# Conversion steps in another order, and transfers moved between and along the issuing queues, in a gated linear attention and SoLU kernel

## The chip, the cores and the metric

The kernel runs on one core of a Trainium2 chip. The metric is the time of one execution on the device in microseconds (us). The kernel before took 368.15 us, the median of three runs (367.41 to 369.79).

A core has five engines that work at the same time, each through its own list of instructions in order: TensorE (PE in the profile, with its weight loads as PEld), VectorE (DVE), ScalarE (ACT), GpSimd (POOL) and SyncE (SP), which here only issues transfers (DMAs). ScalarE can issue transfers too.

## The reference, cut to what matters

```python
# attention: batch 4, heads 8, sequence 768, head dim 48
for t in range(S):
    state = alpha[:, :, t, :, None] * state + np.einsum('bhd,bhe->bhde', k[:, :, t], v[:, :, t])
    y[:, :, t] = np.einsum('bhd,bhde->bhe', q[:, :, t], state)
x = y.transpose(0, 2, 1, 3).reshape(B * S, H * D)          # 3072 tokens x 384
# feed-forward: w_in 384 x 1024, w_out 1024 x 384
h = x @ w_in
e = np.exp(h - h_max)
solu = h * e / (e.sum(-1) + 1e-9)
ln = (solu - mean) / np.sqrt(var + 1e-6) * g_ln
return ln @ w_out
```

The weights `w_in` and `w_out` arrive in float64; all else is float32. The output is float32.

## The kernel before, in words

The sequence of 768 is cut into six groups of 128 tokens, for all four batches at once (`g` 0 to 5). Within a group the recurrence is done in closed form: running products of `alpha` (scans on VectorE) scale the keys one way and the queries the other, `scores` multiplies them on TensorE, `masked` (L289) keeps the causal half, `read_values` (L361) multiplies with v, and `read_state` (L354) adds what the state from the earlier groups contributes. `next_state` and `decay` (L261, GpSimd) carry the state on. The feed-forward of a group is `up` (L397, eight products f = 0 to 7 with blocks of `w_in`), the activation (`up_act`: exponential L411 on ScalarE, product L412 on VectorE, square L415 on ScalarE) and `down` (L516, with `w_out`, two halves for each of four tiles of tokens).

The order of the work on each engine is written out by hand in the program text. Group 0's feed-forward, group 1's attention and the conversion of the weights overlap in the stretch from about 28 to 100 us, and it is this stretch that the change touches.

**Conversion.** Weights come in eight pieces, 0 to 3 of `w_in`, 4 to 7 of `w_out`. `fetch(i, slot)` loads the raw words of piece i into a slot of `room` (L588). `bit(i, k)` does step k of piece i, all on VectorE but one:

- k = 0 (L632) and k = 1 (L636) build the upper part from the high words
- k = 2 (L640) takes its exponent
- k = 3 (L644) brings in the low words, after which the slot is free of VectorE
- k = 4 (L646) adds both into the weights; for piece 7 it is on GpSimd

The list `steps` holds the pairs (i, k) from piece 1 on, and `convert(n)` issues the next n of it. Five go ahead of the products, then after each product f of group 0 as many as its tuple says. Pieces share their work buffers with every second piece. ScalarE checks the range of each piece (`in_range`, L611 and L614), and scales `w_out` with the gains (`scaled`, L653), before `mean` (L667) multiplies it with ones.

**Loads.** `load(alpha, an, 1)` (L134) brings alpha of group 1, which ScalarE's `alpha_over` (L196, both halves) and VectorE's `alpha_T` (L179, L182) read. `load_v(1)` (L176) follows on the same queue.

**Transfers within SBUF.** Queries of group 1 are in two tiles: `qv`, the first 32 of the 48 dimensions of each head, and `qe`, the last 16. `read_state` and `decay` want them in another layout, `q64` (in the tile `lot`). `move_lasts` (L232) does eight transfers from `qe`, issued by SyncE, and `move_firsts` (L237) four from `qv`, issued in group 1 by ScalarE, in later groups by SyncE. The decay of the state (L261) reads the last column of `q64` from both.

The compiler of the program puts a wait on an instruction where it needs another's result. Transfers signal their landing on eight completion counters, shared by all queues, and a transfer also waits until the previous one on its counter has landed.

Of the kernel before, what the change touches and what calls it, by code (L numbers as in the profile page):

```python
# [32 lines left out]
def fast_path(ctx, tc, q, k, v, alpha, moe_w_in, moe_w_out, moe_g_ln, out):  # L33
# [12 lines left out]
    nc = tc.nc  # L46
    B, H, S, D = q.shape
# [6 lines left out]
    E0, E1 = 32, 16  # L54
# [44 lines left out]
    an = const.tile([P, H, TQ, D], FP, name="an")  # L99
    qn = const.tile([P, H, TQ, D], FP, name="qn")  # L100
# [11 lines left out]
    q64 = lot[:, 0 : 2 * H * SW].rearrange("p (c h t) -> p c h t", c=2, h=H)  # L112
# [8 lines left out]
    qv = const.tile([P, 2 * H, SW], FP, name="qv")  # L121
# [9 lines left out]
    def load(src, dst, g):  # L131
        t = slice(g * P, (g + 1) * P)
        for b in range(B):
            nc.sync.dma_start(  # L134
                out=dst[32 * b : 32 * b + 32].rearrange("t h u d -> t h (u d)"),
                in_=src[b, :, t, :].rearrange("h (t u) d -> t h (u d)", u=TQ),
            )
# [5 lines left out]
    def load_first(src, dst, g):  # L143
        t = slice(g * P, (g + 1) * P)
        for b in range(0, B, 2):
            nc.sync.dma_start(
                out=by_token(dst)[:, b : b + 2].rearrange("p b h d -> p (b h) d"),
                in_=src[b : b + 2, :, t].rearrange("b h p d -> p (b h) d"),
            )

    def ends_of(src, tag=None):

        ends = ring.tile([P, T4], FP, name=tag) if isinstance(tag, str) else lots[tag][:, 0:T4]
        ends = ends.rearrange("p (b d) -> p b d", b=B)
        nc.scalar.copy(out=ends.rearrange("p b (h d) -> p b h d", h=H), in_=by_token(src)[:, :, :, E0:D])
        return ends
# [12 lines left out]
    def held(x, n):  # L169

        return x[:, n, 0 : H * HW].rearrange("p (h e) -> p h e", e=HW)[:, :, E1:HW]

    def load_v(g):
        t = slice(g * P, (g + 1) * P)
        for b in range(B):
            nc.sync.dma_start(out=held(vn, b), in_=v[b, :, t, :].rearrange("h p d -> p h d"))  # L176
# [54 lines left out]
            for k in range(2):  # L231
                nc.sync.dma_start(out=q64[64 * i + E0 : 64 * i + 64, c, k::2], in_=qe[32 * b : 32 * b + 32])  # L232

    def move_firsts(queue=nc.sync):
        for b in range(B):
            i, c = divmod(b, 2)
            queue.dma_start(out=q64[64 * i : 64 * i + E0, c], in_=qv[32 * b : 32 * b + 32, 0:H])  # L237

    def ends_of_decay(copy=nc.gpsimd.tensor_copy):
        copy(out=qe[:, :, P:SW], in_=h4[:, H:NB, 1:2])  # L240
# [124 lines left out]
    def next_state(g):  # L365
        kv = banks("kv", [H, D], 2)
        for h in range(H):
            for c in range(2):
                for r in range(4):
                    b = 2 * (r // 2) + c  # L370
                    nc.tensor.matmul(
                        kv[c][quarter(r), h], lhsT=kg[:, b, h, E0 * (r % 2) : E0 * (r % 2) + E0],
                        rhs=vn[:, b, HW * h + E1 : HW * h + HW], start=True, stop=True,
                        tile_position=(0, 32 * r), skip_group_check=True,
                    )
        for c in range(2):
            s = held(state, c)
            if g == 0:
                nc.scalar.copy(out=s, in_=kv[c])
            else:  # L380
                nc.vector.tensor_tensor(out=s, in0=s, in1=kv[c], op=ALU.add)
# [8 lines left out]
    def up_mm(g, f):  # L390
        d = gr[g]
        h = ps_h.tile([P, T4], FP, tag="h", name="h")
        w = T4 if g or f < 2 else T4 // 2 if f == 2 else T4 // 4
        for a in range(KC):
            x = d["x"][:, a].rearrange("p b t -> p (b t)")
            for c in range(0, T4, w):
                nc.tensor.matmul(  # L397
                    h[:, c : c + w], lhsT=w_in[:, a, f * P : (f + 1) * P], rhs=x[:, c : c + w],
                    start=not a and not c, stop=(a == KC - 1), skip_group_check=True,
                )  # L400
        d["h"] = h

    def up_act(g, f, between=None):
        d = gr[g]
        h = d["h"]
        if g:
            e, u2 = (ring.tile([P, T4], FP, name=x) for x in ("e", "u2"))
        else:
            e, u2 = (sT[:, f % 4, 4 * i : 4 * i + 4].rearrange("p b t -> p (b t)") for i in range(2))
        u = u_of(g, f)  # L410
        nc.scalar.activation(out=e, in_=h, func=AF.Exp)  # L411
        nc.vector.tensor_tensor(out=u, in0=h, in1=e, op=ALU.mult)  # L412
        if between:
            between()
        nc.scalar.activation(out=u2, in_=u, func=AF.Square)  # L415
        d[f] = e, u2
# [16 lines left out]
    def array_sums(g, half):  # L433


        d = gr[g]
        if half == 0:
            d["q"] = [ps_a.tile([P, T4], FP, tag=f"a{i}", name=f"quarters{i}") for i in range(2)]
        for i in range(2):
            for f in range(4):  # L440
                r = quarter(f)
                nc.tensor.matmul(
                    d["q"][i][r], lhsT=ones[:, 0:32], rhs=d[4 * half + f][i], start=half == 0, stop=half == 1,
                    tile_position=(0, r.start), skip_group_check=True,
                )
        if half:
            d["p"] = one.tile([P, 2, T4], FP, name="p")
            for i in range(2):
                nc.scalar.copy(out=d["p"][:, i], in_=d["q"][i])
            d["unit"] = small_ones  # L450
# [125 lines left out]
    def fetch(i, slot, n=1):  # L576

        kind, f = pieces[i]
        w = n * F // (2 if kind else KC)
        raw = room[:, 1536 * slot : 1536 * (slot + n)].bitcast(U32)  # L580
        raw = raw.rearrange("p (m c f w) -> p c m f w", m=n, f=w // n, w=2)
        if kind:
            parts = [(slice(0, P), c, moe_w_out[(f + c) * P : (f + c + 1) * P, :]) for c in range(2)]
        else:
            parts = [(slice(0, P), c, moe_w_in[c * P : (c + 1) * P, f * P : f * P + w]) for c in range(KC)]
        for rows, c, src in parts:
            if float64:
                nc.sync.dma_start(  # L588
                    out=raw[rows, c].rearrange("p m f w -> p m (f w)"),
                    in_=src.bitcast(U32).rearrange("p (m x) -> p m x", m=n),  # L590
                )
            else:
                dst = w_out[rows, f + c, 0:DM] if kind else w_in[rows, c, f * P : f * P + w]
                nc.sync.dma_start(out=dst, in_=src)
        for m in range(n):
            raws[i + m] = raw[:, :, m]
# [19 lines left out]
    def bits(steps):  # L616
        for x in steps if float64 else ():
            bit(*x)
# [114 lines left out]
    for i in (0, 2, 1):  # L733
        if i == 1:
# [3 lines left out]
            out=qe[:, :, 0:P] if i == 2 else qv[:, part, 0:P], in0=t[i], in1=aT[:, part, 1:SW], op=ALU.mult  # L738
# [13 lines left out]
    keys_back(0)  # L752
    in_range(0)

    steps = [(1, 0), (1, 1)]
    for i in range(1, 8):
        steps += [(i, 2), (i + 1, 0), (i, 3), (i + 1, 1), (i, 4)]
    steps = [x for x in steps if x[0] < 8]
    for a, b in (((2, 1), (1, 4)), ((6, 1), (5, 4))):
        i, j = steps.index(a), steps.index(b)  # L760
        steps[i], steps[j] = b, a

    def convert(n):
        bits(steps[:n])
        del steps[:n]
# [4 lines left out]
    def check(f):  # L770
        for i, part in checks.get(f, ()):
            in_range(i, (part,))
        if f == FC - 2:
            scaled(4)

    for f in range(FC):
        up_mm(0, f)
        if f == 4:
            array_sums(0, 0)
        up_act(0, f, lambda: check(f))  # L780
        convert((5, 2, 3, 3, 4, 3, 2, 8)[f])
        if f == 0:
            next_state(0)
            fetch(4, 3)
            load(k, kn, 1)
            load_first(q, qn, 1)
        elif f == 1:
            fetch(5, 1)
        elif f == 3:
            fetch(6, 2)  # L790
            load(alpha, an, 1)
            ends_q = ends_of(qn, "u2")
        elif f == 5:
            fetch(7, 3)
            load_v(1)
        elif f == 6:
            scaled(5)
# [34 lines left out]
    for i in range(2):  # L832
        scan_on(1, i)
        part = slice(NP * i, NP * i + NP)
        nc.vector.tensor_tensor(out=qv[:, part, 0:P], in0=tq[i], in1=aT[:, part, 1:SW], op=ALU.mult)  # L835
    move_firsts(nc.scalar)
    down(2, 0)
    scores(1, 0)
    decay(1)
# [6 lines left out]
    masked(1)  # L846
    gr[0]["rest"]()
    finish(0)
    load(q, qn, 2)
    finish(1)  # L850
    finish(2)
    down(3, 0)
# [156 lines left out]
    def compare(out, x, bound, op):  # L1009
# [6 lines left out]
        out=chunks[:, :, 2], in0=sums[:, :, 2], scalar=0.25, in1=sums[:, :, 3], op0=ALU.mult, op1=ALU.is_le  # L1016
# [6 lines left out]
    else:  # L1023
# [9 lines left out]
        out=bad, in0=all_ok[0:1, 0:1], scalar1=float(P * ends[-1]), scalar2=None, op0=ALU.is_lt  # L1033
# [451 lines left out]
```

## Time and profile before

| what | us |
|---|---|
| median of the runs | 368.15 |
| the profiled execution | 368.27 |
| its span, from the first to the last instruction | 366.5 |
| TensorE busy | 355.9 (97%) |
| VectorE busy | 243.7 (67%) |
| ScalarE busy | 146.4 (40%) |
| GpSimd busy | 132.7 (36%) |

In the lines of the timelines below, the first number is the start in us from the span's start and the second the length; then come the engine, the line, the operation, what is written and what is read, the shapes and the number of instructions. A bracket gives the idle time of the engine just ahead, and what ended it. In the list of waits, a line gives the engine, the line that waited and what it waited for, then the total in us, how often, and the longest. `SPq` and `ACTq` are the issuing of transfers by SyncE and ScalarE. The row of busy times has, for each engine, the time, its share of the span and the number of instructions.

### The profile page before, as it was taken

How to read it: one execution, taken by the hardware profiler on the slowest of the kernel's cores; microseconds unless marked ns; L12 is line 12 of the kernel's file. 1: busy time of each engine (PE TensorE's matmuls, PEld its weight loads, DVE VectorE, ACT ScalarE, POOL GpSimd, SP SyncE). 2: the span in 40 equal slices, each digit the busy share in tenths (PEclk: the TensorE clock that was granted, in tenths of full speed). 3: DMA queues.
4: the chain of work that ended last, by engine and by line, in shares of the span. 5: the costliest groups of instructions: out<-in, count | busy, mean ns of one | idle time of the engine just before them, and what ended most of it. 6: DMA issues, size and time to landing. Idle time of an engine off the chain costs nothing. (4 is left out here: it accounts for less than half of the span.)

```text
span 366.5 us, 10048 instructions
## 1 busy us (share of the span) xinstructions
PE 355.9 (97%) x4341; PEld 222.8 (61%) x4341; DVE 243.7 (67%) x381; ACT 146.4 (40%) x261; POOL 132.7 (36%) x128
## 2 busy tenths in 40 slices
PE   8999999988999999999999999999999999999994
PEld 8876896555665566556484556575556565545552
DVE  0999889999987696935765946766956403445420
ACT  2648787327646361252431243531242222322110
POOL 7020002004358673764232763332773120233300
PEclk9999999999999999999999999999999999999999
DMA  9995994723596609354044354004032000000011
GB/s 181 185 323 143 230 253 90 171 53 75 146 208 138 140 6 197 84 131 115 3 109 91 104 113 112 24 26 88 21 88 74 0 25 1 23 21 22 23 47 50
DMA packets 70216, 36.06 MB, mean 98 GB/s; under 512 B 44169, under 2 KB 66961, under 8 KB 70161
## 3 DMA queue, kind: packets, MB, share of 16 engines
q1 hardware_dynamic: 68944, 33.87, 40.3%
q10 hardware_dynamic: 1216, 1.45, 1.4%
q8 instruction: 36, 0.59, 0.7%
q14 instruction: 20, 0.16, 0.1%
HBM read 25.30 MB, written 4.72 MB: 82 GB/s over the span
## 5 line engine op out<-in xcount | busy, mean ns | idle before, releaser
L516 PE MATMUL o<-w_out,room 128*128 128x385 f32 x384 | 133.4, 491 | 0.0
L397 PE MATMUL h<-x,w_in 128*128 128x512 f32 (+2 forms) x384 | 132.1, 490 | 0.0
L516 PEld LDWEIGHTS o<-w_out,room 128*128 128x128 f32 x384 | 71.3, 190 | 55.1 <-issue 13.2
L397 PEld LDWEIGHTS h<-x,w_in 128*128 128x128 f32 x384 | 62.4, 190 | 50.6 <-issue 41.8
L412 DVE TENSOR_TENSOR room<-h,e 128x512 f32<-128x512 f32 x40 | 27.7, 691 | 74.0 <-ACT e L411 74.0
L411 ACT ACTIVATE e<-h 128x512 f32<-128x512 f32 x40 | 23.9, 598 | 100.3 <-PE h L397 100.3
L430 POOL TENSOR_TENSOR p<-p,e 128x512 f32<-128x512 f32 x30 | 43.1, 1437 | 20.0 <-ACT e L411 19.9
L415 ACT ACTIVATE u<-room 128x512 f32<-128x512 f32 x40 | 25.2, 630 | 35.2 <-DVE room L412 35.2
L555 POOL TENSOR_TENSOR r<-sums,mhalf 128x1 f32<-128x1 f32 x20 | 14.8, 741 | 66.3 <-DVE sums L546 66.0
L289 DVE TENSOR_TENSOR sT<-a,mask 128x512 f32<-128x512 f32 x43 | 26.7, 686 | 6.8 <-PE a L278 6.7
L204 DVE TENSOR_TENSOR_SCAN hT<-aT,unit 128x516 f32<-128x516 f32 x18 | 24.3, 1400 | 7.9 <-ACT aT L719 7.9
L225 POOL TENSOR_TENSOR kT<-kT,hT 128x1024 f32<-128x1024 f32 (+1 forms) x8 | 13.3, 1684 | 33.5 <-DVE kT L179 33.5
L278 PEld LDWEIGHTS a<-qv,kT 32*128 32x128 f32 x704 | 20.8, 186 | 7.6 <-issue 2.4
L204 DVE TENSOR_TENSOR_SCAN aT<-aT,seed 128x516 f32<-128x516 f32 x18 | 24.8, 1407 | 0.2
L430 DVE TENSOR_TENSOR p<-p,u 128x512 f32<-128x512 f32 x30 | 21.5, 717 | 5.1 <-ACT u L415 5.1
L333 PE MATMUL y<-sT,vn 128*32 128x128 f32 x768 | 23.4, 274 | 0.9 <-issue 0.7
L278 PE MATMUL a<-qv,kT 32*128 32x128 f32 x704 | 23.2, 277 | 1.1 <-DVE qv L835 0.8
L333 PEld LDWEIGHTS y<-sT,vn 128*32 128x32 f32 x768 | 20.9, 110 | 2.9 <-issue 2.2
L196 ACT ACTIVATE sq<-an,mone 128x1536 uint8<-128x1536 f32 x12 | 18.9, 1571 | 0.2
L557 ACT ACTIVATE o_sb<-o,r 128x384 f32<-128x384 f32 x16 | 9.3, 580 | 18.5 <-POOL r L555 18.5
L646 POOL TENSOR_TENSOR w_out<-lot 128x768 f32<-128x768 f32 x1 | 1.8, 1847 | 37.2 <-DVE lot L644 37.2
L261 POOL TENSOR_TENSOR state<-state,lot 128x384 f32<-128x384 f32 x10 | 8.8, 900 | 16.7 <-DMA lot<-qe 13.3
(148 smaller groups left out, 378.0 us busy)
## 6 DMA issues: line engine op xcount, KB each, us to landing
vn<-in_v_dram SPq DMA_DIRECT2D x24, 192.0 KB, 4.6
kn<-in_k_dram SPq DMA_DIRECT2D x20, 192.0 KB, 4.9
an<-in_alpha_dram SPq DMA_DIRECT2D x20, 192.0 KB, 4.2
out_dram<-o_sb SPq DMA_DIRECT2D x20, 192.0 KB, 1.9
room<-in_moe_w_out_dram SPq DMA_DIRECT2D x8, 384.0 KB, 6.0
qn<-in_q_dram SPq DMA_DIRECT2D x16, 192.0 KB, 3.5
lot<-qe SPq DMA_DIRECT2D x40, 64.5 KB, 2.1
lot<-qv SPq DMA_DIRECT2D x16, 129.0 KB, 2.4
```

Of the source, the lines that this page charges most:

```text
L196: nc.scalar.activation(out=sq, in_=x, func=AF.Relu, scale=1.0 - 2 * i, bias=mone, accum_out=over[:, g, i : i + 1])
L204: nc.vector.tensor_tensor_scan(out=o, data0=a, data1=s, initial=1.0, op0=ALU.mult, op1=ALU.add)
L278: nc.tensor.matmul(a[b][:, i], lhsT=kT[quarter(b), kb], rhs=qv[quarter(b), qb, 0:P], start=not last and not i, stop=bool(last), tile_posit ...
L289: nc.vector.tensor_tensor(out=sT[:, b, half * NP : half * NP + NP], in0=a[b], in1=mask[:, None, :].to_broadcast([P, NP, P]), op=ALU.mult,)
L333: nc.tensor.matmul(y_bank(b)[quarter(r), a], lhsT=lhsT, rhs=rhs, start=(b, r) not in begun, stop=stop, tile_position=(row, 32 * r), skip_g ...
L397: nc.tensor.matmul(h[:, c : c + w], lhsT=w_in[:, a, f * P : (f + 1) * P], rhs=x[:, c : c + w], start=not a and not c, stop=(a == KC - 1), ...
L411: nc.scalar.activation(out=e, in_=h, func=AF.Exp)
L412: nc.vector.tensor_tensor(out=u, in0=h, in1=e, op=ALU.mult)
L415: nc.scalar.activation(out=u2, in_=u, func=AF.Square)
L430: eng.tensor_tensor(out=p, in0=d[0][i] if f == 1 else p, in1=d[f][i], op=ALU.add)
L516: nc.tensor.matmul(d["o"][:, 0 : DM + 1], lhsT=u_of(g, f)[:, b * P : b * P + P], rhs=w_out[:, f], start=(f == 0), stop=(f == FC - 1), skip ...
L555: nc.gpsimd.tensor_tensor(out=r, in0=s[:, 3:4], in1=mhalf, op=ALU.pow)
```

## The change

Four things. The list of conversion steps is written out in a new order, and the numbers of steps per product go from (5, 2, 3, 3, 4, 3, 2, 8) to (5, 2, 3, 4, 3, 3, 3, 7). In steps per product, where 43 is piece 4 with k = 3:

| behind product | before | after |
|---|---|---|
| 3 | 41 34 42 | 41 34 42 43 |
| 4 | 50 43 51 44 | 44 50 51 |
| 5 | 52 60 53 | 52 60 53 |
| 6 | 54 61 | 54 61 62 |
| 7 | 62 70 63 71 64 72 73 74 | 63 70 71 64 72 73 74 |

Those ahead are the same. Second, alpha's load for group 1 goes from behind `fetch(6, 2)` (product 3) to behind `fetch(7, 3)` (product 5). Third, `move_firsts` of group 1 is issued by SyncE. Fourth, the load of the queries of group 2 goes from behind the first output's transfer (`finish(0)`) to just behind `move_firsts`.

```diff
-    def move_firsts(queue=nc.sync):
+    def move_firsts():
         for b in range(B):
             i, c = divmod(b, 2)
-            queue.dma_start(out=q64[64 * i : 64 * i + E0, c], in_=qv[32 * b : 32 * b + 32, 0:H])
+            nc.sync.dma_start(out=q64[64 * i : 64 * i + E0, c], in_=qv[32 * b : 32 * b + 32, 0:H])
...
-    steps = [(1, 0), (1, 1)]
-    for i in range(1, 8):
-        steps += [(i, 2), (i + 1, 0), (i, 3), (i + 1, 1), (i, 4)]
-    steps = [x for x in steps if x[0] < 8]
-    for a, b in (((2, 1), (1, 4)), ((6, 1), (5, 4))):
-        i, j = steps.index(a), steps.index(b)
-        steps[i], steps[j] = b, a
+    steps = [10, 11, 12, 20, 13, 14, 21, 22, 30, 23, 31, 24, 32, 40, 33, 41, 34, 42, 43, 44, 50, 51, 52, 60, 53, 54, 61, 62]
+    steps = [divmod(x, 10) for x in steps + [63, 70, 71, 64, 72, 73, 74]]
...
-        convert((5, 2, 3, 3, 4, 3, 2, 8)[f])
+        convert((5, 2, 3, 4, 3, 3, 3, 7)[f])
...
         elif f == 3:
             fetch(6, 2)
-            load(alpha, an, 1)
             ends_q = ends_of(qn, "u2")
         elif f == 5:
             fetch(7, 3)
+            load(alpha, an, 1)
             load_v(1)
...
-    move_firsts(nc.scalar)
+    move_firsts()
+    load(q, qn, 2)
     down(2, 0)
     scores(1, 0)
     decay(1)
...
     gr[0]["rest"]()
     finish(0)
-    load(q, qn, 2)
     finish(1)
     finish(2)
```

## The prediction, made before the result was known

> **What bounds the kernel now.** I read the page first, then TensorE's own timeline from 24 to 100 us (the change touches nothing outside), then the timelines of the engines that TensorE waits for there, and last SyncE's waits.
>
> ```profile
> PE 355.9 (97%) x4341; PEld 222.8 (61%) x4341; DVE 243.7 (67%) x381; ACT 146.4 (40%) x261; POOL 132.7 (36%) x128
> ...
> 73.43 0.66 PE L303 MATMUL tp<-ident,kT 128*128 128x128 f32 x4 [0.92 <-DVE kT L817]
> 73.92 2.76 PE L516 MATMUL o<-w_out,room 128*128 128x385 f32 x8
> 77.50 2.07 PE L278 MATMUL a<-qv,kT 32*128 32x128 f32 x64 [0.82 <-DVE qv L835]
> ...
> 84.28 2.86 PE L516 MATMUL o<-w_out,room 128*128 128x385 f32 x8
> 87.52 0.55 PE L333 MATMUL y<-lot,state 64*32 64x128 f32 x16 [0.38 <-POOL state L261]
> 88.75 1.02 PE L333 MATMUL y<-lot,state 64*32 64x128 f32 x48 [0.68 <-POOL aT L188]
> 89.70 1.56 PE L516 MATMUL o<-w_out,room 128*128 128x385 f32 x4
> ```
>
> Columns: start, length, then in brackets the idle time ahead and what ended it. TensorE is the bound. From 24 to 72.5 us it has no gap, so whatever becomes faster there buys nothing there. Its stalls sit in three places: 0.92 us before the last key transposes, 0.82 us before the scores, and around `read_state(0)`. The third is priced by starts. From 84.28 to 89.70 pass 5.42 us; the same `down` elsewhere lasts 2.76 (73.92 to 76.68) and `read_state` 1.26 from start to start (123.65 to 124.91 in the next group), 4.02 in all, so the stall is 1.40 us. Together 3.14 us: **the most that the change can win here**.
>
> The first two stalls end with VectorE, which works through `keys_T(1)` to `masked(1)` almost without a pause from 61.56 us. So what counts is when it gets there, and the conversion ahead has pauses:
>
> ```profile
> 45.43 0.69 DVE L412 TENSOR_TENSOR room<-h,sT 128x512 f32<-128x512 f32 x1 [0.71 <-ACT sT L411]
> 46.87 0.56 DVE L632 TENSOR_SCALAR lot<-room 128x768 uint32<-128x768 uint32 x1 [0.75 <-DMA room<-in_moe_w_out_dram]
> ...
> 55.57 0.69 DVE L412 TENSOR_TENSOR room<-h,sT 128x512 f32<-128x512 f32 x1 [0.80 <-ACT sT L411]
> 56.18 0.55 DVE L640 TENSOR_SCALAR lot<-lot 128x768 uint32<-128x768 uint32 x1
> 57.00 0.56 DVE L632 TENSOR_SCALAR lot<-room 128x768 uint32<-128x768 uint32 x1 [0.26 <-DMA room<-in_moe_w_out_dram]
> ...
> 61.56 2.19 DVE L179 STREAM_TRANSPOSE kT<-kn 128x1024 f32<-128x1024 f32 x1
> ```
>
> The third stall ends with GpSimd's `decay(1)`, which waits for transfers within SBUF:
>
> ```profile
> 75.64 10.64 SPq L232 DMA_DIRECT2D lot<-qe  x8
> 79.38 2.53 ACTq L237 DMA_DIRECT2D lot<-qv  x4
> 86.63 0.84 POOL L261 TENSOR_TENSOR state<-state,lot 128x384 f32<-128x384 f32 x1 [12.93 <-DMA lot<-qe]
> 87.86 0.84 POOL L261 TENSOR_TENSOR state<-state,lot 128x384 f32<-128x384 f32 x1 [0.39 <-DMA lot<-qe]
> ...
> SPq L232 <- DMA lot<-qv: 5.4, 1, 5.4
> ```
>
> Of `move_lasts`' eight issues the first is at 75.64 and the second only at 81.79: SyncE sits 5.4 us until the first of ScalarE's `move_firsts` has landed (79.38 + 2.4). The two write different partitions; the wait is on a completion counter. The program of before has eight of these for all transfers, dealt out in the order in which it expects the transfers to start, and a transfer waits for its counter's previous user. `move_firsts` got its counters first.
>
> **What the Trainium skill says.** Perfetto Trace Analysis, Identifying the Most-Contended Engine: matmul busy share misleads, since matmuls are pipelined. Agreed: TensorE shows as 97% busy and the `read_state` stall shows as 1.06 us of gaps where starts give 1.40; I use starts. DMA: Bandwidth & Descriptors, Issuing engines are not separate DMA queues: ScalarE's and SyncE's transfers share the same engines, and a second issuer saves issue time only. Agreed: `lot<-qv` lands after a median 2.4 us from either queue. Same page, Anatomy of one DMA: a semaphore wait is served by the issuing sequencer before dispatch. Agreed: all seven later `move_lasts` stood behind the second's wait. SBUF — State Buffer, Who interferes with whom: a VectorE operation with two SBUF inputs is held up by a GpSimd one that reads SBUF. Agreed: L543 took 0.72 us instead of 0.16 and ended with the second decay, at 88.71.
>
> **The change, part by part.** Starts follow each other on VectorE by 0.47 us for L632 and L640, 0.87 for L636, L644 and L646 (40.16, 40.63; 42.43, 43.30, 44.17), and by 0.60 for L412. I name steps by piece and k.
>
> (1) *Steps.* No instruction more or less: 43 goes from behind product 4 to behind product 3, 44 then stands ahead of 50, 62 goes from behind 7 to behind 6, and 63 ahead of 70. Behind product 3, 43 fills the 0.71 us pause: it starts at 44.63 and ends its 0.87 at 45.50, so L412 of product 4 slips from 45.43 to 45.5. Then 44 (to 46.97), 50 without its 0.75 us wait, since its data landed at 46.8, 51, done at 48.3. Product 5's L412 now waits for its exponential (49.14) and starts at 49.17 instead of 49.96. Steps 52, 60, 53 end at 51.6; product 6's exponential is ScalarE's and stays (52.03), so the lead shrinks: L412 at 52.06 instead of 52.36. 54, 61, 62 end at 54.87; `scaled(5)` waits for 54 and starts 0.3 earlier, so product 7's exponential ends at 55.22, and L412 is at 55.25. Before, 70, 63, 71, 64, 72, 73 took 4.56 (57.00 to 61.56, 74 being GpSimd's); the same six, in their new order and with no wait for 70, now start at 55.85. `keys_T(1)` starts at 60.41: **1.15 us earlier**.
>
> (2) *alpha behind w_out's last.* Piece 7 goes into piece 4's room, so its load waited for 43 (48.30); now 43 ends at 45.6 and ScalarE's range check of piece 4 at 46.3. It is issued at 46.3 instead of 48.36. Alpha's four follow at about 47.1 to 49 instead of 43.71 to 46.7; behind them on SyncE only `load_v(1)`, from 49.3 as before, needed after 90. The engines are full in these slices (DMA share about 1), so bytes come in order: before, alpha's last landed at 45.64 + 9.6 = 55.2 and w_out's last at 48.75 + 8.2 = 57.0. Exchanged, w_out's is there by about 53.5 (70 needs it at 56.7) and **alpha at about 57.0**. Its first reader is `alpha_over` on ScalarE, at 56.5: it waits 0.5 us. Behind it there are the copies of p, `scaled(6)` and `scaled(7)`. TensorE wants p at 61.0 and the last scaled rows at 64.7; from alpha's landing these take 1.75 + 1.05 = 2.8 and about 6.7 us, so alpha may land as late as 58.0 at no cost. I take nothing; beyond 58.0 it is us for us.
>
> (3) *All within SBUF by SyncE.* The eight lasts go at 0.65 us each, as in the next group (112.41 to 117.58): from 74.5 (VectorE's lead) to 79.7. The four firsts wait for L835's second, 79.30 less 1.15, so they follow at once, at 0.6 to 0.8 each (3.23 for four in the next group), and land by 83.6 (third) and 84.6. `decay(1)` ends at 84.5 and 85.5 instead of 87.47 and 88.70. TensorE, itself 1.15 earlier, gets to `read_state(0)` at 85.9: **the 1.40 us go**, with 0.7 to spare. ScalarE loses its 3.7 us wait and 2.5 us of issues; it had idle time there, so nothing. What is late next: nothing behind the firsts but the queries' load.
>
> (4) *Next queries' load.* Four issues move from 91.02 to about 82.5, behind the firsts; its first reader is at 97.83, so no gain, and the outputs' issues no longer stand behind it. If it met the firsts' packets it could cost `decay` some tenths, which the 0.7 cover.
>
> *Sum.* The key stall: 0.92 shrinks to nothing. TensorE then stands before the scores until VectorE's 76.35 instead of 77.50: 1.15 won in all by there (0.59 of the 0.82 stays). Plus 1.40: 2.55 us. VectorE must follow: its 1.15, and 0.56 of L543's hold-up, give 1.7 at 100 us, with a pause of 0.71 ahead of L412 at 101.54 to spare; enough. One term works against: `decay(2)` ends at 123.92 and TensorE reads at 123.65, nothing to spare. Its chain begins with alpha's third load behind ScalarE's `alpha_over`, which follows TensorE, so it moves along; it may give back 0 to 0.5 us. I take 0.1.
>
> The profiled execution took 368.27 us, of which the span is 366.5. 366.5 - 2.45 = 364.05 span, 365.8 with the 1.77 around it; the median of the runs is 0.12 below the profiled one, so **about 365.7 us**, 0.7% less.
>
> **Rivals.** (A) *Half of it*: the conversion lead is eaten by ScalarE (its order, not VectorE's, sets products 6 and 7), or the firsts on SyncE come too late for `decay(1)`, or `decay(2)` takes back what is won. For it: the lead already shrinks from 0.79 to 0.30 at product 6, and the 0.7 us margin. Against: the removed waits for data are real. Gain 0.9 to 1.5: 367.0. (B) *Slower*: alpha lands late. Its packets share the engines with v's, issued right behind, and `alpha_over` blocks ScalarE, thus p, the row sums on TensorE, then `scaled(7)` and the mean of w_out. It costs from 58.0 on and outweighs the gain from 60.5 on; at 61.5, where v's own last now lands (60.1) and somewhat beyond, the loss is 1.0: 369.2. Against it: v is queued behind alpha, and w_out's last, in the same place before, was not held up past 57.0. (C) *More*: VectorE's lead is over 1.7 us, so that the score stall goes too: 3.1 us, 365.1. Against: ScalarE's exponentials. That the change doesn't do what it says can't be, save that the counters are dealt out anew: were the lasts again to wait for later transfers, (A).
>
> **Chances.** Forecast (gain 1.7 to 2.9) 0.62; A 0.22; B 0.08; C 0.08. The forecast's own range, with 0.5 us for the median of a few runs, is 364.6 to 366.9. To leave out no more than 2 in 10 it reaches to A's end and some of C: 364.3 to 367.8. One per cent, about what tells a change from none here, is 3.7 us, more than all three stalls; only C with luck in the runs gets there: faster 0.08, slower 0.03, the same 0.89.
>
> **What would show it.** Right: `keys_T(1)` at 60.2 to 60.7; no wait ahead of L303's last four; the lasts in one row of 5.2 us and the firsts behind, from SyncE; `decay(1)` over before TensorE's L333; TensorE's first L397 of the next group, 98.14 before, at about 95.6. Wrong: `alpha_over` starting after 58; a wait of SyncE within the lasts; an L333 that waits for `state` near 86 or 121.

## The result, and the profile after

| | before | after |
|---|---|---|
| median of 8 runs each, us | 368.41 | 365.19 |
| lowest to highest, us | 366.42 to 369.79 | 364.67 to 365.89 |
| the profiled execution, us | 368.27 | 364.92 |
| its span, us | 366.5 | 363.1 |

The ratio after to before is 0.9919, with a 95% interval of 0.9893 to 0.9945: 0.8% faster, where 0.7% was forecast (365.7 us, range 364.3 to 367.8). The interval has 1% in it.

The first part of the page of the kernel after, engine by engine:

```profile
PE 354.5 (98%) x4341; PEld 221.8 (61%) x4341; DVE 243.4 (67%) x381; ACT 146.4 (40%) x261; POOL 132.8 (37%) x128
```

No engine has more or fewer instructions than before. What changed is when TensorE stood. Its own timeline:

```profile
71.07 1.66 PE L303 MATMUL tp<-ident,kT 128*128 128x128 f32 x12
72.57 2.76 PE L516 MATMUL o<-w_out,room 128*128 128x385 f32 x8
76.15 2.07 PE L278 MATMUL a<-qv,kT 32*128 32x128 f32 x64 [0.82 <-DVE qv L830]
...
82.93 2.86 PE L516 MATMUL o<-w_out,room 128*128 128x385 f32 x8
85.72 1.16 PE L333 MATMUL y<-lot,state 64*32 64x128 f32 x64
86.82 1.56 PE L516 MATMUL o<-w_out,room 128*128 128x385 f32 x4
```

The twelve key transposes are one row now: the bracket ahead of the last four is gone. The 0.82 us ahead of the scores stands, to the hundredth. And `read_state(0)` (L333) follows the `down` ahead of it with no bracket.

To compare kernels, I take differences between starts on TensorE in one execution. The landmarks are: the first sums over the products (L442, "product sums" below and "first down" in the expectations of e9 to e11; their start is the zero, since all of TensorE's work before it is untouched by the change), the `down` behind the key transposes, the scores, the `down` ahead of `read_state(0)`, the one behind it, the one behind `read_values`, and the L397 behind `read_state` of group 2.

| stretch, us | before | after | difference |
|---|---|---|---|
| product sums to `down` behind key transposes | 30.21 | 29.25 | -0.96 |
| on to the scores | 3.58 | 3.58 | 0 |
| on to the `down` ahead of `read_state(0)` | 6.78 | 6.78 | 0 |
| on to the `down` behind it | 5.42 | 3.89 | -1.53 |
| on to the `down` behind `read_values` | 7.04 | 6.49 | -0.55 |
| on to L397 behind `read_state` of group 2 | 28.17 | 28.45 | +0.28 |
| all | 81.20 | 78.44 | -2.76 |

The last matmuls start 3.29 us earlier (353.46 to 350.17). Of the rest, 0.39 us was there before the first changed instruction ran (L442 at 43.71 and 43.32), and so is no work of the change.

VectorE's timeline, the conversion steps up to the transposes of the keys:

```profile
44.37 0.96 DVE L644 SCALAR_TENSOR_TENSOR lot<-room,lot 128x768 f32<-128x768 uint32 x1
45.24 0.68 DVE L412 TENSOR_TENSOR room<-h,sT 128x512 f32<-128x512 f32 x1
...
48.78 0.69 DVE L412 TENSOR_TENSOR room<-h,sT 128x512 f32<-128x512 f32 x1 [0.53 <-ACT sT L411]
...
51.66 0.69 DVE L412 TENSOR_TENSOR room<-h,sT 128x512 f32<-128x512 f32 x1 [0.38 <-ACT sT L411]
...
54.89 0.69 DVE L412 TENSOR_TENSOR room<-h,sT 128x512 f32<-128x512 f32 x1 [0.20 <-ACT sT L411]
...
60.20 2.18 DVE L179 STREAM_TRANSPOSE kT<-kn 128x1024 f32<-128x1024 f32 x1
```

The two pauses for w_out's data, 0.75 and 0.26 us, are gone. Step 43 (44.37) fills the pause ahead of L412, and what is left are three short waits for ScalarE's exponential. The key transposes start at 60.20 instead of 61.56; from the product sums it is 16.88 instead of 17.85 us, so 0.97 earlier.

Then SyncE's and GpSimd's timelines:

```profile
74.29 5.43 SPq L232 DMA_DIRECT2D lot<-qe  x8
79.83 2.47 SPq L237 DMA_DIRECT2D lot<-qv  x4
82.81 1.98 SPq L134 DMA_DIRECT2D qn<-in_q_dram  x4
...
83.61 1.65 POOL L261 TENSOR_TENSOR state<-state,lot 128x384 f32<-128x384 f32 x2 [11.26 <-DMA lot<-qv]
```

The eight lasts took 10.64 us to issue and now take 5.43. The decay ends at 85.26, TensorE's first L333 is at 85.72: 0.46 us apart. One of the eight took 0.77 us to issue where its neighbours take 0.60; such long issues come up again below.

### The profile page after: what moved, and what is told of

Same layout as the page of the kernel before. It is cut to its first block, busy times and chain, and to the rows that moved or that the text cites. A ratio compares the mean times of both kernels' runs of the same rounds, so it can differ in the third digit from the quotient of the medians.

```text
span 363.1 us, 10050 instructions
## 1 busy us (share of the span) xinstructions
PE 354.5 (98%) x4341; PEld 221.8 (61%) x4341; DVE 243.4 (67%) x381; ACT 146.4 (40%) x261; POOL 132.8 (37%) x128
## 5 line engine op out<-in xcount | busy, mean ns | idle before, releaser
L397 PE MATMUL h<-x,w_in 128*128 128x512 f32 (+2 forms) x384 | 132.3, 490 | 0.6 <-issue 0.6
L397 PEld LDWEIGHTS h<-x,w_in 128*128 128x128 f32 x384 | 62.4, 190 | 51.4 <-issue 41.4
L412 DVE TENSOR_TENSOR room<-h,e 128x512 f32<-128x512 f32 x40 | 27.7, 694 | 72.7 <-ACT e L411 72.7
L333 PE MATMUL y<-sT,vn 128*32 128x128 f32 x768 | 22.9, 273 | 0.2 <-DVE sT L289 0.2
L333 PEld LDWEIGHTS y<-sT,vn 128*32 128x32 f32 x768 | 20.8, 110 | 1.8 <-issue 1.2
```

The source lines that it names most:

```text
L333: nc.tensor.matmul(y_bank(b)[quarter(r), a], lhsT=lhsT, rhs=rhs, start=(b, r) not in begun, stop=stop, tile_position=(row, 32 * r), skip_g ...
L397: nc.tensor.matmul(h[:, c : c + w], lhsT=w_in[:, a, f * P : (f + 1) * P], rhs=x[:, c : c + w], start=not a and not c, stop=(a == KC - 1), ...
```

## The experiments

All eleven, with before and after for comparison. Times of stretches are TensorE's, in us, as above; "all" goes from the product sums to L397 behind `read_state` of group 2.

| kernel | to `down` behind keys | to scores | around `read_state(0)` | to `down` behind `read_values` | all | ratio to before, 95% interval |
|---|---|---|---|---|---|---|
| before | 30.21 | 3.58 | 5.42 | 7.04 | 81.20 | |
| after | 29.25 | 3.58 | 3.89 | 6.49 | 78.44 | 0.9919 (0.9893 to 0.9945) |
| e1_sync_only | 30.69 | 3.57 | 3.89 | 6.77 | 79.94 | 0.9953 (0.9930 to 0.9977) |
| e2_steps_alpha | 29.23 | 3.57 | 4.11 | 6.21 | 78.52 | 0.9935 (0.9910 to 0.9960) |
| e3_swapped | 30.04 | 3.57 | 4.30 | 6.21 | 79.61 | 0.9977 (0.9960 to 0.9994) |
| e4_queries_back | 29.21 | 3.57 | 3.92 | 7.62 | 79.31 | 0.9931 (0.9903 to 0.9958) |
| e5_alpha_back | 29.22 | 3.57 | 4.11 | 6.80 | 78.65 | 0.9924 (0.9896 to 0.9952) |
| e6_alpha_only | 29.60 | 3.57 | 4.12 | 6.44 | 78.87 | 0.9945 (0.9918 to 0.9971) |
| e7_alpha_behind_v | 29.62 | 3.29 | 4.03 | 7.94 | 79.66 | 0.9924 (0.9895 to 0.9954) |
| e8_steps_earlier | 29.06 | 2.80 | 3.89 | 7.92 | 78.66 | 0.9913 (0.9878 to 0.9947) |
| e9_steps_queries_early | 29.06 | 2.78 | 4.16 | 6.38 | 77.71 | 0.9911 (0.9897 to 0.9926) |
| e10_queries_early | 29.20 | 3.57 | 5.03 | 6.25 | 79.23 | 0.9945 (0.9925 to 0.9966) |
| e11_steps_queries_back | 29.06 | 2.77 | 3.88 | 6.70 | 77.61 | 0.9908 (0.9889 to 0.9927) |

Two things limit how this is read. A stretch is from one execution. And the start of the product sums itself lies anywhere from 43.02 (e10) to 45.65 us (e9), though the work ahead is the same; whole runs of one kernel spread by 1.2 us (after) to 5.1 us (before, in the group of runs with e5 to e8).

For the lead the executions can be set against each other. Before, e1 and e3 have the old order of steps with alpha in its old place, and their first stretch is 30.21, 30.69 and 30.04 us. After, e2, e4, e5 and e10 have the new order with alpha ahead of v, and it is 29.25, 29.23, 29.21, 29.22 and 29.20. So the gain in this stretch is no accident of one execution, and its size is between 0.8 and 1.5 us.

### Which part removes which stall: e1 and e2

Theory: the stall at `read_state(0)` goes with the firsts' queue alone, and the lead with the steps (and alpha). e1 is the kernel before with one line changed:

```diff
-    move_firsts(nc.scalar)
+    move_firsts()
```

> The kernel before with only the issuer of the firsts changed: the four transfers of move_firsts in group 1 go by SyncE, all else stays. Our theory (two separate gains): the eight lasts go in one row of about 5.2 us without SyncE's 5.4 us wait, decay(1) is over before TensorE comes to read_state(0), and the stretch from the start of down's half ahead of read_state(0) to the start of the half behind it shrinks from 5.42 to about 3.9 us (3.89 in the kernel after). The 0.92 us wait ahead of the last key transposes and the 0.82 ahead of the scores stay. Time 1.5 us (0.4%) below before. Rival (the stall goes because VectorE is earlier): that stretch stays above 5 us and the time is that of before.

TensorE and GpSimd in e1:

```profile
74.13 0.66 PE L303 MATMUL tp<-ident,kT 128*128 128x128 f32 x4 [0.81 <-DVE kT L817]
...
84.97 2.86 PE L516 MATMUL o<-w_out,room 128*128 128x385 f32 x8
87.77 1.17 PE L333 MATMUL y<-lot,state 64*32 64x128 f32 x64
88.86 1.56 PE L516 MATMUL o<-w_out,room 128*128 128x385 f32 x4
...
85.89 1.64 POOL L261 TENSOR_TENSOR state<-state,lot 128x384 f32<-128x384 f32 x2 [11.49 <-DMA lot<-qv]
```

The key stall stays (0.81), and the stretch around `read_state(0)` is 3.89 instead of 5.42: the queue alone takes the whole stall away. The time is 366.88 against 367.99.

Its first stretch is 0.48 us longer than in before though nothing is changed there; 0.33 us of that is a wait of TensorE for VectorE's L412 at 51.74, and VectorE was late because it had waited 1.57 us for w_out's data, where in before it waited 0.75.

e2 has the other half, the kernel before with the new list of steps (as in the change above), the new numbers per product and alpha's load behind `fetch(7, 3)`:

```diff
-        convert((5, 2, 3, 3, 4, 3, 2, 8)[f])
+        convert((5, 2, 3, 4, 3, 3, 3, 7)[f])
...
             fetch(6, 2)
-            load(alpha, an, 1)
...
             fetch(7, 3)
+            load(alpha, an, 1)
```

> The kernel after with its two last parts undone: new order of the steps and alpha's load behind w_out's last, but the firsts by ScalarE and the queries' load in its old place. Our theory: keys_T(1) about 1 us earlier, the 0.92 us wait ahead of the last key transposes gone, the wait before the scores still there, down ahead of read_state(0) 1.0 us earlier. The counters are dealt out a little differently here (the wait for a first falls on the fourth of the lasts, not the second), so the stretch around read_state(0) is between 4.2 and 5.4 us. Time 1.0 to 2.0 us below before. Rival (ScalarE's order eats the lead): keys_T(1) less than 0.5 us earlier and no measurable gain.

The lead is there (29.23 against 30.21) and the score wait stays. But most of the stall at `read_state(0)` is gone too (4.11, a little under the expected 4.2), with the firsts still on ScalarE, and the gain between medians is 2.1 us. SyncE's timeline, then a line of its waits:

```profile
74.75 9.33 SPq L232 DMA_DIRECT2D lot<-qe  x8
...
SPq L232 <- DMA lot<-qv: 4.1, 1, 4.1
```

SyncE still waits for a first, 4.1 us instead of 5.4. But it now has three lasts out before (the fourth is issued at 80.90), where before it had one. With alpha's load elsewhere in the order, the compiled program deals out the eight counters differently, and the wait falls on the fourth last. The kept traces give the counter of each transfer: in before the second last has the same one as the first of the firsts (105), in e2 the fourth last has it (107). The decay ends at 86.49, only a little after TensorE's 86.18.

### Counters, or two queues at once: e3

That wait might come from the firsts sharing the engines with the lasts, or from ScalarE issuing slowly. e3 swaps the queues in the kernel before: ScalarE issues the lasts, SyncE the firsts.

```diff
-    move_lasts()
+    move_lasts(nc.scalar)
...
-    move_firsts(nc.scalar)
+    move_firsts()
```

> The kernel before with issuers exchanged in group 1: the eight lasts by ScalarE, the four firsts by SyncE; so two queues still issue, and ScalarE issues even more, but the lasts now have their counters ahead of the firsts. If the stall of before comes from the counters' order: the lasts go back to back at about 0.65 us from 77 us on, none waits for a first, decay(1) ends near 85.5 us, and the stretch around read_state(0) is about 3.9 to 4.2 us; time about 1.4 us below before. If it comes from two queues at work at once or from ScalarE as an issuer: the lasts or firsts are slowed, decay(1) ends at 87 or later, the stretch stays near 5.4 and the time is that of before.

ScalarE's timeline, a line of SyncE's waits, and GpSimd's timeline:

```profile
75.89 0.74 ACTq L232 DMA_DIRECT2D lot<-qe  x1
76.67 5.19 ACTq L232 DMA_DIRECT2D lot<-qe  x7
...
SPq L237 <- DMA lot<-qe: 1.3, 2, 0.9
...
84.92 1.65 POOL L261 TENSOR_TENSOR state<-state,lot 128x384 f32<-128x384 f32 x2 [11.02 <-ACT sq L611]
```

With two queues issuing at the same time, none of the lasts waits for a first. Now it is SyncE's firsts that wait for a last, although they write other partitions. So it isn't the second queue as such that held the lasts; a wait between transfers without shared data does. The decay is over at 86.57, later than the expected 85.5, but still 0.72 us before TensorE comes to it (87.29). The stretch is 4.30 all the same, 0.41 over e1's; why that row of L333 is longer isn't settled. The gain, 0.64 us between medians, is below the expected 1.4; another of SyncE's transfers, alpha's for group 2, met such a wait too (7.3 us for a last), without a stall of TensorE that the profile shows.

### The load of the next queries: e4

```diff
-    load(q, qn, 2)
     down(2, 0)
...
     finish(0)
+    load(q, qn, 2)
```

> The kernel after with only the queries' load of group 2 put back behind the first output. Our forecast had given this part nothing; the traces show read_state(1) and read_values shorter by 0.55 us after the change (from 7.04 to 6.49 us from the start of down behind read_state(0) to the start of down behind read_values). If the load's packets are what held TensorE up there: that stretch goes back to about 7.0 us, and the time is 0.5 us above after. If that was an accident of one execution, or comes from read_state(0)'s earlier end: it stays near 6.5 and the time is that of after within 0.3.

The time is 366.15. By the medians that is 1.0 us above after, by the ratios to before 0.4, and the intervals overlap for most of their width: no effect of this part is shown, and one of some tenths isn't excluded. The stretch came to 7.62, above both expectations. Its trace has one odd line, on TensorE at the end of `read_values`:

```profile
94.73 0.38 PE L333 MATMUL y<-sT,vn 128*32 128x128 f32 x2 [1.03 <-issue]
```

A pause of 1.03 us in which TensorE waited for nothing that the profile shows; without it the stretch would be 6.59, near after's 6.49. I come back to it below.

### Alpha's load: e5, e6 and e7

e5 is after with alpha's load back behind `fetch(6, 2)`, e6 is before with only alpha's load moved, e7 is after with alpha put behind v as well:

```diff
             fetch(7, 3)
-            load(alpha, an, 1)
             load_v(1)
+            load(alpha, an, 1)
```

> The kernel after with only alpha's load put back behind piece 6, ahead of piece 7. Our theory: the lead of VectorE comes from the order of the steps, which frees piece 4's room 2 us sooner; with alpha's four loads ahead of it, piece 7 lands at 55 to 56.5 us instead of 51, just as 70 wants it (56.4), so from the start of L442 (product sums) to the start of down behind the key transposes pass 29.25 to 29.6 us (30.21 before, 29.25 after), and the time is that of after, 0 to 0.4 us more. Rival (alpha's place carries the lead): 70 waits for its data, that stretch is 29.8 or more, and the time is 0.6 us or more above after.

> The kernel before with only alpha's load moved behind piece 7. Our theory: VectorE gains no more than the 0.26 us wait of 70 (the stretch from L442 to down behind the key transposes is 29.9 to 30.3 us, 30.21 before). But moving four transfers deals the completion counters out anew: in this program the wait for a first falls on the fourth of the lasts and not on the second, as in the run of steps and alpha, so the stretch around read_state(0) shrinks from 5.42 to about 4.1 to 4.4 us. Time 1.0 to 1.5 us below before. Rival (decay's stall depends on when VectorE is ready, or on who issues): that stretch stays above 5 us and the time is that of before.

> The kernel after with alpha's load one place further back, behind v's. This prices rival B of the prediction. Alpha is then issued from about 56 us and lands near 61 to 62; alpha_over, on ScalarE, which started at 56.15, waits until then; behind it there are the copies of p, scaled(6) and scaled(7). By the prediction's slack (no cost up to 58.0 in before's times, 57.6 in after's, then us for us) TensorE stands still before the row sums (L465) and before the mean (L667), about 4 us in all: from the start of L442 to the start of down behind the key transposes pass about 33 us instead of 29.25, and the time is 3.5 to 4.5 us above after, thus about 1 us above before. If the slack were larger than thought: less than 2 us above after.

**e5**: the lead is the same as in after (29.22; the key transposes 16.88 us behind the product sums in both). On top of the new order of steps, alpha's place brings nothing. No kernel has the new order and nothing else; e5 against e1, which differ in it and in the queries' load, is the nearest.

**e6**: alone, alpha's place brings 0.61 us up to the key transposes, more than expected: VectorE no longer waits for w_out's data. The pieces land 3.3 to 6.0 us after their issue instead of 4.4 to 8.2, and the first of them is issued 3.85 us ahead of the product sums instead of 2.96. And `read_state(0)` takes 4.12, once more with one wait on the fourth last:

```profile
75.29 9.34 SPq L232 DMA_DIRECT2D lot<-qe  x8
...
SPq L232 <- DMA lot<-qv: 4.1, 1, 4.1
```

The gain between medians is 1.8 us, above the expected 1.0 to 1.5. So both halves of the change, and alpha alone, each remove most of the same stall. The gains of e1 and e2 in the two stretches may not be added.

**e7** puts a price on the rival that alpha comes late. ScalarE's timeline:

```profile
55.81 0.64 ACT L415 ACTIVATE sT<-room 128x512 f32<-128x512 f32 x1 [0.76 <-DVE room L412]
58.70 1.58 ACT L196 ACTIVATE sq<-an,mone 128x1536 uint8<-128x1536 f32 x1 [2.25 <-DMA an<-in_alpha_dram]
60.28 1.05 ACT L449 COPY p<-quarters 128x512 f32<-128x512 f32 x2
```

`alpha_over` does wait 2.25 us, and TensorE loses 0.37 up to the key transposes against after. But there VectorE was to stop it anyway: the stretch to the scores shrinks from 3.58 to 3.29, so 0.08 us are left. The time is 365.39, as after. My expectation of 3.5 to 4.5 us was far off; v's issues took 4.75 us instead of the 7 and more on which it rested, so alpha was there at 58.6 and not at 61 to 62. A landing as late as that was not run.

### What bounds next: e8 to e11

After VectorE's lead of 0.97 us the scores still wait 0.82 us. e8 gives VectorE the rest by moving one more step ahead:

```diff
-        convert((5, 2, 3, 4, 3, 3, 3, 7)[f])
+        convert((5, 2, 3, 4, 4, 3, 3, 6)[f])
```

> The kernel after with the same order of steps dealt out one step earlier: four behind product 4, three behind 5, 6, and six behind 7 (52 behind product 4, 54 behind 5, 63 behind 6). In after VectorE still pauses 0.53 us ahead of L412 of product 5, 0.38 ahead of product 6's and 0.20 ahead of product 7's, and TensorE still waits 0.82 us before the scores for VectorE. If VectorE's pauses are what is left to win: keys_T(1) starts 0.7 to 0.9 us earlier against L442 (16.0 to 16.2 us behind its start instead of 16.88), the wait before the scores is gone or under 0.2 us, and the time is 0.6 to 0.9 us below after. If ScalarE's exponentials set the pace of products 6 and 7: L412 of product 7 is as late as in after, and the gain is under 0.3 us.

TensorE in e8:

```profile
72.29 2.76 PE L516 MATMUL o<-w_out,room 128*128 128x385 f32 x8
75.09 2.07 PE L278 MATMUL a<-qv,kT 32*128 32x128 f32 x64
...
87.26 1.12 PE L333 MATMUL y<-lot,state 64*32 64x128 f32 x61
89.62 0.41 PE L333 MATMUL y<-lot,state 64*32 64x128 f32 x3 [1.24 <-issue]
```

The score wait is gone, 0.97 us are won by there, and 1.24 us go again in `read_state(1)`, with the same kind of pause as in e4. The median is 365.07, not the expected 0.6 to 0.9 below after. Is it the load of the queries, running beside it, that causes this? e9 and e10 take that load far ahead, behind the transposes of group 1's queries, e9 on top of e8 and e10 on top of after. e11 is e8 with the load put back as in e4.

```diff
     turned(qn, ends_q, tq)
+    load(q, qn, 2)
...
     move_firsts()
-    load(q, qn, 2)
```

> As the run with more steps earlier (44 behind product 4, 62 ahead of 70 as before; starts of VectorE's key transposes 15.9 us behind the first down), and the load of group 2's queries moved to right behind the transposes of group 1's queries, so that SyncE issues it near 67 to 73 us and no load runs while TensorE is in read_state(1) and read_values. Theory (the 1.24 us pause of TensorE in read_state(1), ended by nothing that the profile shows, comes from that load's packets beside TensorE's instruction fetch): no such pause from 80 to 97 us; from the first down to the first L397 behind read_state of group 2 it takes 77.4 us (78.66 less 1.24), and the time is 364.0 us, 1.1 below the run before it. Rival (the pause comes at this place whatever else is loading): 0.2 to 1.2 us of pause are still there, 78.2 to 78.7 us, time 365. A second rival: the load now stands ahead of the lasts on SyncE and delays them; then the first last is later than 73.3 us and read_state(0) waits for the decay, 0.3 to 1 us.

> The kernel after with only the load of group 2's queries moved to right behind the transposes of group 1's queries. The kernel after has no pause of TensorE in read_state(1), so theory and rival both say: the 12 stretches from 69 to 95 us as in the kernel after (first down to scores 32.8 us, down to down around read_state(0) 3.9), first down to first L397 behind read_state of group 2 78.2 to 78.7, time 365.0 to 365.4. If the load's packets do set the pause, it is absent here too; if a pause of 0.5 us or more shows up, they don't.

> More steps earlier, and the load of group 2's queries in its old place behind the first output's transfer (near 88 us). Theory (that load's packets set the pause): no pause in read_state(1), which is over by then, but one of 0.5 to 1.2 us within read_values or the down behind it, as the run with the load alone put back had (1.03 us). Rival (the place in TensorE's own instruction stream sets it): a pause in read_state(1) of about 1.2 us as with the load early. First down to first L397 behind read_state of group 2: 78.4 to 78.8 by both; time 365.

Neither e9 nor e10 has such a pause in this place, and their stretches to the `down` behind `read_values` are short (6.38, 6.25). But e2 and e3 have the shortest of all, 6.21, with the load in its old place, and e11, also with the load there, shows 6.70 and no flagged pause, against both of its expectations. So the load's place alone doesn't settle it.

The packets of the kept traces say more. The page of after lists a queue of another kind:

```profile
q8 instruction: 36, 0.59, 0.7%
```

These are 36 transfers of 16 KB each. TensorE's pauses without a releaser come at a few places, the same in every kernel: behind 478, 604 and 732 matmuls in the start-up, behind 1368 or 1369 at the end of `read_state(1)` and behind 1497 at the end of `read_values`. From one place to the next it is about 128 matmuls, or five times that. The views flag 20 such pauses in the 13 kernels, and each ends 1.26 to 1.61 us after a q8 transfer has landed. At these five places of 13 kernels, TensorE paused in all 18 cases in which its work ahead ended less than 1.2 us behind the landing, in none of the 40 in which it ended more than 1.4 us behind, and in some of the 7 between. In e8 the transfer landed at 88.07, the work ahead ended at 88.38 and TensorE went on at 89.62; in after these are 87.42 and 89.43, without a pause. These cases point to one cause: TensorE stands until a late transfer of instructions has landed. No run was made to test it, and what makes a transfer late **stays open**. The queries' load is a suspect: at the last two places 6 of 11 cases with this load beside the transfer pause (one of them, in e5, for 0.13 us and not flagged), and none of 15 without it.

e9 and e11 win about 0.8 us over after in the whole stretch (77.71 and 77.61 against 78.44). Their medians, 365.07 and 364.98 us, can't be told from after's 365.19 by these runs, nor can their ratios; e9 was expected at 364.0. e8 and e11 differ as after and e4 do, in the queries' load alone, and there the kernel with the load in its old place has the shorter stretch.

e10 missed in another way. GpSimd's and TensorE's lines:

```profile
85.86 0.55 PE L333 MATMUL y<-lot,state 64*32 64x128 f32 x16 [0.43 <-POOL state L261]
...
84.97 1.64 POOL L261 TENSOR_TENSOR state<-state,lot 128x384 f32<-128x384 f32 x2 [12.98 <-DMA lot<-qv]
```

Its eight lasts took 6.11 us to issue, one of them 1.46 instead of 0.60, one of the firsts 1.05, and the decay came too late: 5.03 instead of 3.89. After has its longest issue at 0.77. That is how thin the cover over `read_state(0)` is. The median is 366.38, where 365.0 to 365.4 was expected.

## Why the prediction was right, and where not

- **Lead of VectorE (forecast 1.15 us).** Right in kind, 0.97 in size. The mis-sized term is the pitch: I let steps follow each other by 0.47 us for L632 and L640, read where the step behind doesn't read what that step wrote. In the new order 43 stands directly behind 42, 51 behind 50, and 71 behind 70; those pairs start 0.59 to 0.61 apart (43.78 to 44.37, 46.71 to 47.30, 56.36 to 56.97), and 62 is 0.99 behind 61 instead of 0.87. Most of this is swallowed where VectorE then waits for ScalarE's exponential, with 0.53, 0.38 and 0.20 us: against the product sums L412 of products 5 and 6 comes within 0.01 us of the forecast, that of product 7 within 0.03. What is lost is lost behind it. I let the last six steps take the 4.56 us of before, but there 63 stood between 70 and 71; they take 4.70 (55.50 to 60.20).
- **Key and score stalls.** The first went; of the second I had 0.59 left and it is 0.82, by the 0.18 of missing lead and by TensorE's own 0.96 instead of 0.92. Together the two were forecast at -1.15, measured -0.96.
- **Stall at `read_state(0)` (forecast 1.40).** It went whole, 1.53 by starts. The 1.26 us that I took for an undisturbed `read_state`, from group 2, was not undisturbed: there the decay ended 0.27 us behind TensorE. Undisturbed it is 1.10 (85.72 to 86.82). e1 shows that the queue suffices for it; e2 and e6 show that dealing out the counters anew by another edit does nearly the same, and this I had only as a way in which the change could fail. The forecast had the decay over at 85.5 and TensorE there at 85.9. These two leave 0.4 us of cover; the 0.7 that it stated comes out only if TensorE wants the second half of the decayed state 16 matmuls into its row, where the row of before breaks, and that step isn't written there. Measured are 85.26 and 85.72, so 0.46, and 0.70 to the 17th matmul (85.96). e5 (decay over at 86.44, TensorE at 86.12) and e10 show it used up.
- **Alpha's load (forecast nothing, landing at 57.0).** Its last was issued at 48.24 and landed 7.4 later, at 55.6, and `alpha_over` (56.15) did not wait. The forecast that w_out's last would gain by the exchange held (51.0; I had 53.5), but no step waits for it: e5 has the same lead with alpha in its old place. "Bytes come in order" was too strict: the last transfer of piece 6, issued ahead of alpha, took 6.6 to 7.8 us to land in the four kernels with alpha's load directly behind it (before, e1, e3, e5), and 4.0 to 6.3 in the nine others.
- **Queries' load (forecast nothing).** Neither shown nor refuted: e4 doesn't resolve it, and the pair e8 and e11 points the other way.
- **Give-back at `decay(2)` (forecast 0.1).** Wrong place. `read_state` of group 2 got 0.16 shorter. What was given back, 0.43 us, is in the two passes of scores of group 2, which took 2.29 and 2.14 us instead of 2.00; no wait is shown there, and I didn't test it. On the other side stand 0.55 us between `read_state(0)` and the `down` behind `read_values`, forecast at nothing: a pause of 0.24 in before, of e4's kind, and shorter matmul rows.
- **The sum.** Forecast -2.45 us of span, measured -2.76 in the stretch and -3.4 in the span with the earlier start. By medians it is -3.22, with an interval of about -3.9 to -2.0. That the sum came so near is in part luck: the 0.55 won and the 0.43 given back that nobody forecast nearly cancel.
- **The rivals.** (A), half of it: no step failed by that much. (B), alpha late: in e7 alpha came 0.6 us later than the 58.0 and TensorE lost 0.08 us by the scores. Its price, us for us beyond 58.0, left out that VectorE would have stopped TensorE at the scores anyway. (C), score stall gone too: not in this change; e8 shows that a further step does it.

## What to carry to other kernels

Where a queue stands on a transfer that shares no data with it, suspect what signals completions before bandwidth: look which transfer it waits for, and in which order the program expects them to be issued. Gains from edits that remove the same wait in different ways don't add, so an edit is priced by undoing it alone and by doing it alone (e5 and e6 differ). And a stage that ends on another engine a few us later absorbs a delay put ahead of it, as in e7, and a lead as well: ask what is left of it at the next place where two engines meet.

## What was not expected of the hardware

- A transfer that waits for an unrelated one cost 5.4 us of issue, and moving a load issued 30 us earlier changed which transfer it struck (e2, e6: the second became the fourth).
- TensorE pauses of 0.18 to 1.24 us, with no releaser in the profile, at the end of `read_state(1)` or `read_values`: 0.24 in before, 0.18 in e1, 1.03 in e4, 0.99 in e7, 1.24 in e8, none flagged in the others. Such pauses also stand ahead of all changed work: 0.46 at 24 us in before, 0.58 at 35 us in after, 2.22 in two pauses from 31 to 37 us in e9, none in e10. All 20 end 1.26 to 1.61 us after a 16 KB transfer on the queue of kind instruction has landed.
- On VectorE a step that reads what the one directly ahead wrote starts about 0.12 us later than one that doesn't (0.59 against 0.47 behind L632 and L640, 0.99 against 0.87 behind L636).
- Most transfers within SBUF take 0.60 us to issue and follow each other by 0.65. In each of the ten kernels whose lasts go out in one row, one takes 0.77 (after) to 1.57 us (e5). It is one that starts while a q8 transfer is under way, and its issue ends 0.39 to 0.43 us after that transfer does, in all ten. So the cover over `read_state(0)` hangs on where these two meet; why the issue waits isn't shown.
